# Spreading weight sums over chunks and moving the second transpose or hash behind the third pair of scores, in a hash-attention and feed-forward kernel

## The chip, the cores and the metric

One core of a Trainium2 chip. The metric is the device time of one execution in microseconds; medians of several runs are quoted.

PE is the matmul engine, PEld its weight load, DVE the vector engine, ACT the scalar engine, POOL GpSimd, SP the engine that issues most DMAs. In the views, `sc` are the scores, `tp_q` and `tp_k` the transposes of q and k, `hs` the hashes, `sm` the totals, `st` the transpose of the totals (L708), `accd` and `accp` the sums of probabilities on VectorE and on GpSimd, `pt` the exps.

## The reference, cut to what matters

```python
# q, k, v: (4, 8, 768, 64); proj: (64, 6); w_in (512, 2048), w_out (2048, 512)
mask   = q_bucket[:, :, :, None] == k_bucket[:, :, None, :]   # 6-bit hashes by proj
scores = where(mask, q @ k.T / sqrt(64), -1e9)
attn   = exp(scores - max);  attn /= sum(attn) + 1e-9
x      = (attn @ v) as (3072, 512)
h      = x @ w_in
out    = (max(h, 0) + alpha * min(h, 0)) @ w_out
```

## The kernel before: the parts that matter

Attention runs in 32 chunks `u` of 384 queries for a pair of heads. Beside its own work each chunk prepares one piece of the weights (`weight_*`, on DVE) and, for the next pair of heads, transposes (`turn`, even chunks) or hashes (`hash_bits`, odd chunks).

```python
    def weight_group(i):                     # every 4th piece of w_in, every 2nd of w_out
        ...
        for to, a, c in sums4:               # four sums in one block
            do(DVE.tensor_tensor(w[:, to], w[:, a], w[:, c], op=ALU.subtract))
        ... dma_start(w_in_s or w_out_s, w)

    def add_first(u):  do(POOL.tensor_tensor(accp[u], p(u, 0), p(u, 1), op=ALU.add))
    def add_third(u):  do(POOL.tensor_tensor(accp[u], accp[u], p(u, 2), op=ALU.add))
    def add_last(u):
        do(DVE.tensor_tensor(accd[u], p(u, 3), p(u, 4), op=ALU.add))        # L674
        do(DVE.tensor_tensor(accd[u], accd[u], p(u, 5), op=ALU.add))        # L675
        do(DVE.tensor_tensor(accd[u], accd[u], accp[u], op=ALU.add))        # L676

    for u in range(UNITS):
        scores(u, 0); add_first(u)
        if u > 0: add_last(u - 1)
        turn(pi+1,"q",0), turn(pi+1,"q",1)   or  hash_bits(pi+1, 0)
        if u > 0: attend(u - 1, 0)
        weight_parts(u)                      # L552 L553 L556 L557 on DVE
        scores(u, 1); add_third(u)
        weight_sum(u); weight_group(u)       # L577 L582, then the block L599
        turn(pi+1,"k",0), turn(pi+1,"k",1)   or  hash_bits(pi+1, 1)
        if u > 0: attend(u - 1, 1); totals(u - 1)
        scores(u, 2)
        if u > 0: divide(u - 1)              # begins with L708, the transpose of the totals
        load_weight(u + 3)
        if u == HW: load_w(0); load_w(1); load_x(0); sums_x(0)    # HW = 16; four sums on POOL
        ...
```

`turn`, `hash_bits` and `totals` take turns in two PSUM buffers named "mi"; one allocated to totals is free again when L708 has read it. The rest of the kernel (products with the feed-forward weights, after about 410 us) is not touched.

## Time and profile before

| | before |
|---|---|
| median | 997.81 us (997.47 to 998.15, 4 runs) |
| attention stage | about 20 to 410 us |
| DVE busy in chunks 1 to 15 | 170.37 of 178.83 us |
| PE busy in the same | 174.57 us |
| a chunk | 11.8 us, or 12.6 where a block of sums holds PE up |

What PE waits for, in the stage from 20 to 412 us (columns: total us, times, longest):

```profile
PE sm L698 <- DVE accd L676: 7.7, 6, 3.0
PE sc L653 <- ACT pt L658: 5.5, 30, 0.4
PE tp_q L614 <- DVE st L708: 2.7, 6, 0.6
```

Some 16 us in 390: PE's waits are small because PE is nearly full. And here are seven VectorE groups in that stage (busy us, mean ns; last the idle time before):

```profile
L676 DVE TENSOR_TENSOR accd<-accd,accp 128x768 f32<-128x768 f32 x32 | 53.4, 1667 | 3.3
L675 DVE TENSOR_TENSOR accd<-accd,pt 128x768 f32<-128x768 f32 x32 | 43.7, 1364 | 3.3
L674 DVE TENSOR_TENSOR accd<-pt,pt 128x768 f32<-128x768 f32 x32 | 40.3, 1260 | 0.0
L553 DVE TENSOR_SCALAR wx<-wx 128x512 uint32<-128x512 uint32 x31 | 35.9, 1158 | 1.1
L577 DVE SCALAR_TENSOR_TENSOR wr<-wx,wr 128x512 f32<-128x512 f32 x31 | 27.0, 872 | 1.1
L557 DVE SCALAR_TENSOR_TENSOR wr<-raw,wr 128x512 f32<-128x512 uint32 x31 | 23.0, 741 | 1.1
L556 DVE TENSOR_SCALAR wr<-wx 128x512 uint32<-128x512 uint32 x31 | 14.7, 475 | 1.1
```

These seven rows take 238.0 us, and the mean of the first four is far above the shortest of their kind. What is above it is time in which the engine counts as busy and stands still.

### The profile page before, as it was taken

Reading aid. Unit: us, or ns where it says so; the run is one execution under the profiler, and the core shown is the slowest. Engines: PE = TensorE matmul, PEld = TensorE weight load, DVE = VectorE, ACT = ScalarE, POOL = GpSimd, SP = SyncE. Lnnn points to the kernel's source line nnn. Section 1 sums busy time; section 2 is a strip of 40 time slices with the busy share of each in tenths; the row PEclk is TensorE's granted clock in tenths of the full one; section 3 lists DMA queues with packets and bytes.
Section 4 is the critical chain, followed back from the end, with each engine's and each line's share of the span. In section 5 each row is a group of like instructions: output and inputs, shape, how many; then the busy total and the mean of one; then the engine's idle time right before and its main releaser. Section 6 shows DMA issues by size and latency. Waiting matters only on the chain.

```text
span 998.3 us, 12489 instructions
## 1 busy us (share of the span) xinstructions
PE 963.2 (96%) x4741; PEld 594.0 (60%) x4741; DVE 605.8 (61%) x959; ACT 371.0 (37%) x669; POOL 158.5 (16%) x98
## 2 busy tenths in 40 slices
PE   6999999989999998999999999999999999999997
PEld 3444444434444443455788655888656888556886
DVE  3999999999999999766600366500467300665100
ACT  6777676665777664222100122100222000222000
POOL 2333333262333333000300000300000300000000
PEclk9999999998999999999999999999999999999999
DMA  7465756355444431463400133300224200231000
GB/s 199 126 182 143 237 154 179 107 164 157 143 143 143 127 111 53 200 259 110 137 22 22 58 111 99 123 22 21 71 88 155 68 22 22 84 111 37 22 22 24
DMA packets 93316, 106.81 MB, mean 107 GB/s; under 512 B 53296, under 2 KB 79936, under 8 KB 93248
## 3 DMA queue, kind: packets, MB, share of 16 engines
q1 hardware_dynamic: 91680, 105.54, 33.1%
q8 instruction: 39, 0.64, 0.3%
q10 hardware_dynamic: 1568, 0.39, 0.2%
q14 instruction: 29, 0.24, 0.1%
HBM read 78.65 MB, written 27.26 MB: 106 GB/s over the span
## 4 chain that ended last, share of the span: by engine, by line
PE 61%; DVE 35%; ACT 1%; issue 1%; DMA 1%; DVEq 0%; SPq 0%; ACTq 0%
PE z_2a L756 6%; PE z_1a L756 6%; PE z_0a L756 6%; DVE accd L676 5%; DVE accd L675 4%; DVE accd L674 4%; DVE wx L553 3%; PE z_1c L756 3%; PE z_0c L756 3%; PE z_2c L756 3%; DVE wr L577 2%; DVE wr L557 2%; PE f_2a L756 2%; PE f_3a L756 2%; PE f_7a L756 2%; PE f_6a L756 2%
## 5 line engine op out<-in xcount | busy, mean ns | idle before, releaser
L658 ACT ACTIVATE pt<-sc 128x768 f32<-128x768 f32 x192 | 149.9, 813 | 119.8 <-PE sc L653 119.8
L653 PE MATMUL sc<-qT,kT 64*128 64x384 f32 x768 | 157.5, 487 | 0.0
L686 PE MATMUL av<-pt,vn 128*64 128x385 f32 (+1 forms) x768 | 138.1, 495 | 0.0
L667 POOL TENSOR_TENSOR accp<-pt,pt 128x768 f32<-128x768 f32 x32 | 62.0, 1939 | 222.5 <-ACT pt L658 185.2
L686 PEld LDWEIGHTS av<-pt,vn 128*64 128x64 f32 x768 | 49.4, 136 | 72.6 <-issue 72.6
L732 POOL TENSOR_TENSOR x<-x,x 128x768 f32<-128x768 f32 x16 | 31.9, 2005 | 364.0 <-DMA x<-x_s 363.4
L810 DVE TENSOR_TENSOR g<-g,g 128x384 f32<-128x384 f32 x128 | 82.5, 665 | 2.2
L653 PEld LDWEIGHTS sc<-qT,kT 64*128 64x128 f32 x768 | 69.8, 190 | 15.3 <-issue 15.2
L653 PEld LDWEIGHTS <-kb 64*128 64x128 bf16 x384 | 24.4, 94 | 79.3 <-issue 62.7
L653 PE MATMUL sc<-qb,kb 64*128 64x384 bf16 x384 | 64.6, 329 | 5.6 <-ACT pt L658 5.6
L670 POOL TENSOR_TENSOR accp<-accp,pt 128x768 f32<-128x768 f32 x32 | 62.3, 1946 | 39.0 <-ACT pt L658 38.9
L756 PE MATMUL z_2a<-wo,g 128*128 128x256 f32 x256 | 58.0, 379 | 0.5 <-ACT z_2u L763 0.5
L756 PE MATMUL z_1a<-wo,g 128*128 128x256 f32 x256 | 57.9, 379 | 0.0
L756 PE MATMUL z_0a<-wo,g 128*128 128x256 f32 x256 | 57.9, 379 | 0.0
L676 DVE TENSOR_TENSOR accd<-accd,accp 128x768 f32<-128x768 f32 x32 | 53.4, 1667 | 3.3
L803 DVE SCALAR_TENSOR_TENSOR g<-h,alpha 128x384 f32<-128x384 f32 x32 | 22.1, 692 | 54.4 <-ACT h L795 54.4
L756 PEld LDWEIGHTS z_2a<-wo,g 128*128 128x128 f32 x256 | 48.6, 190 | 8.1 <-ACT z_2u L763 0.9
L756 PEld LDWEIGHTS z_0a<-wo,g 128*128 128x128 f32 x256 | 48.6, 190 | 7.5
L756 PEld LDWEIGHTS z_1a<-wo,g 128*128 128x128 f32 x256 | 48.6, 190 | 6.6
L675 DVE TENSOR_TENSOR accd<-accd,pt 128x768 f32<-128x768 f32 x32 | 43.7, 1364 | 3.3
L674 DVE TENSOR_TENSOR accd<-pt,pt 128x768 f32<-128x768 f32 x32 | 40.3, 1260 | 0.0
L639 ACT ACTIVATE qb<-hs,hb 32x384 bf16<-32x384 f32 x64 | 36.7, 574 | 2.2 <-PE hs L636 1.0
(217 smaller groups left out, 1477.1 us busy)
## 6 DMA issues: line engine op xcount, KB each, us to landing
wi<-w_in_s SPq DMA_DIRECT2D x32, 896.0 KB, 4.6
raw<-in_moe_w_in_dram SPq DMA_DIRECT2D x16, 512.0 KB, 4.1
raw<-in_moe_w_out_dram SPq DMA_DIRECT2D x16, 512.0 KB, 3.6
w_in_s<-wsi SPq DMA_DIRECT2D x16, 448.0 KB, 5.4
w_out_s<-wso SPq DMA_DIRECT2D x8, 896.0 KB, 4.4
wo<-w_out_s SPq DMA_DIRECT2D x8, 896.0 KB, 7.4
qn<-in_q_dram SPq DMA_DIRECT2D x32, 192.0 KB, 3.7
vn<-in_v_dram SPq DMA_DIRECT2D x16, 384.0 KB, 4.4
```

Of the source, the lines that this page charges most:

```text
L639: do(ACT.activation(bits["q", pi][D * s : D * s + 32, cols], ps[r], AF.Sign, bias=hb[r]))
L653: do(PE.matmul(sc[:, s, :CW], what["k", pi][r, ks], what["q", pi][r, qs], start=first, stop=not first,))
L658: do(ACT.activation(pt[:, :, :CW], sc[:, :, :CW], AF.Exp, scale=SCALE / DOWN))
L667: do(POOL.tensor_tensor(accp[u], p(u, 0), p(u, 1), op=ALU.add))
L670: do(POOL.tensor_tensor(accp[u], accp[u], p(u, 2), op=ALU.add))
L674: do(DVE.tensor_tensor(accd[u], p(u, 3), p(u, 4), op=ALU.add))
L675: do(DVE.tensor_tensor(accd[u], accd[u], p(u, 5), op=ALU.add))
L676: do(DVE.tensor_tensor(accd[u], accd[u], accp[u], op=ALU.add))
L686: do(PE.matmul(av[u][D * s : D * s + D, :w], nat["v", pi][:, s, kc * D : (kc + 1) * D], prob[u, kc][:, s, :w], start=(kc == 0), stop=(kc = ...
L732: do(POOL.tensor_tensor(x_m[b, to], x_m[b, a], x_m[b, c], op=ALU.subtract))
L756: do(PE.matmul(self.ps[bank], self.left(left, k), self.right(right, k), start=start and k == 0, stop=k == self.nk - 1, skip_group_check=no ...
L810: do(DVE.tensor_tensor(g_m[to, i], g_m[x, i], g_m[y, i], op=op))
```

## The change

The intent: no block of four sums that holds VectorE, and so L708 and PE, for 2.7 us at a time; and work for PE between the third pair of scores and the next chunk's first, where it waits for the exps.

```diff
+    sums_due = []
     def weight_group(i):
         ...
-        for to, a, c in sums4:
-            do(DVE.tensor_tensor(...))
-        ... dma_start(...)
+        for x in sums4:
+            sums_due.append((one, x))        # one(): the same tensor_tensor
+        sums_due.append((store, ()))         # store(): the same dma_start
+    def weight_sums(count):
+        while sums_due and (count or sums_due[0][0].__name__ == "store"):
+            fn, x = sums_due.pop(0)
+            count -= fn.__name__ == "one"
+            fn(*x)
@@ in the loop over chunks
         weight_sum(u)
+        weight_sums(1 if u < HW else 2)
         weight_group(u)
-        if more:
-            turn(pi + 1, "k", 0), turn(pi + 1, "k", 1)  or  hash_bits(pi + 1, 1)
         ... attend, totals, scores(u, 2), divide(u - 1)
+        if more:
+            turn(pi + 1, "k", 0), turn(pi + 1, "k", 1)  or  hash_bits(pi + 1, 1)
         load_weight(u + 3)
-        if u == HW:
+        if u == HW + 2:
             load_w(0); load_w(1); load_x(0); sums_x(0)
@@ after the loop
     divide(last)
+    weight_sums(4)
```

More of the change, by code (lines that the diff above doesn't have):

```diff
@@ L597, in weight_group, with one, store @@
             return
-        for to, a, c in sums4:
+        def one(to, a, c):
             do(DVE.tensor_tensor(w[:, to], w[:, a], w[:, c], op=ALU.subtract))
-        if i < HW:
-            c, kk = divmod(n, 2)
-            for ii in range(4):
-                nc.sync.dma_start(w_in_s[4 * c + ii][:, :, kk], w[:, :, ii])
-        else:
-            nc.sync.dma_start(w_out_s[n], w)
+        def store():
+            if i < HW:
+                c, kk = divmod(n, 2)
+                for ii in range(4):
+                    nc.sync.dma_start(w_in_s[4 * c + ii][:, :, kk], w[:, :, ii])
+            else:
+                nc.sync.dma_start(w_out_s[n], w)
+        for x in sums4:
[6 more added lines that the diff above has]
+            fn(*x)
     def turn(pi, name, half):
@@ L893, in fast_path @@
         weight_sum(u)
+        weight_sums(1 if u < HW else 2)
         weight_group(u)
-        if more:
-            if g == 0:
-                turn(pi + 1, "k", 0)
-                turn(pi + 1, "k", 1)
-            else:
-                hash_bits(pi + 1, 1)
         if u > 0:
@@ L908, in fast_path @@
             divide(u - 1)
+        if more:
+            if g == 0:
+                turn(pi + 1, "k", 0)
+                turn(pi + 1, "k", 1)
+            else:
+                hash_bits(pi + 1, 1)
         load_weight(u + 3)
-        if u == HW:
+        if u == HW + 2:
             load_w(0)
```

## The prediction

> **What bounds the kernel now.** I read the page's chain first, then busy time by stage, then the groups of VectorE (DVE), and last the timeline of a few chunks. A chunk (`u`, 32 of them) is half the queries of one pair of heads; even chunks transpose the next pair's q and k ("turn"), odd ones hash them.
>
> The chain that ended last, by engine:
>
> ```profile
> PE 61%; DVE 35%; ACT 1%; issue 1%; DMA 1%; DVEq 0%; SPq 0%; ACTq 0%
> ```
>
> 35% of 998 us is about 350 us, as long as the attention stage (from 20 to 410 us). Past 410 us the chain is matmuls back to back, and the change does nothing there. Busy time in four stretches of attention (columns: PE, PEld, DVE, ACT, POOL busy, granted clock, DMA share, GB/s); the second is the one where x is first loaded and summed:
>
> ```profile
> 25.27:204.10 178.83, 174.57 (x1168) 77.39 (x1166) 170.37 (x245) 127.94 (x212) 57.33 (x30) 1.00 0.56 160
> 204.10:246.66 42.56, 38.82 (x242) 17.17 (x240) 40.73 (x54) 24.37 (x42) 20.07 (x11) 0.92 0.55 163
> 246.66:391.85 145.19, 139.49 (x920) 60.37 (x918) 138.25 (x209) 99.00 (x162) 47.43 (x24) 1.00 0.40 126
> 391.85:412.00 20.15, 17.85 (x92) 7.43 (x89) 18.18 (x30) 4.14 (x6) 4.00 (x2) 1.00 0.17 66
> ```
>
> The first row is 15 chunks of 11.92 us, the third 12 chunks of 12.10. DVE and PE are both at 95% or more, so both are near the bound. DVE's busy time is not all work, though:
>
> ```profile
> L676 DVE TENSOR_TENSOR accd<-accd,accp 128x768 f32<-128x768 f32 x31 | 52.4, 1690 | 3.2
> L553 DVE TENSOR_SCALAR wx<-wx 128x512 uint32<-128x512 uint32 x31 | 35.9, 1158 | 1.1
> L599 DVE TENSOR_TENSOR wso<-wso 128x256 f32<-128x256 f32 x28 | 11.9, 425 | 1.0
> L599 DVE TENSOR_TENSOR wsi<-wsi 128x512 f32<-128x512 f32 x16 | 10.7, 691 | 0.4
> ```
>
> L676 has a mean of 1690 ns and L553 of 1158 ns, although single ones take 957 and 430. The timeline shows what stretches them, and where PE waits:
>
> ```profile
> 96.22 1.81 POOL L667 TENSOR_TENSOR accp<-pt,pt 128x768 f32<-128x768 f32 x1 [7.10 <-ACT pt L658]
> 96.30 2.54 DVE L676 TENSOR_TENSOR accd<-accd,accp 128x768 f32<-128x768 f32 x1
> ...
> 99.24 1.69 POOL L670 TENSOR_TENSOR accp<-accp,pt 128x768 f32<-128x768 f32 x1 [1.21 <-ACT pt L658]
> ...
> 99.48 1.73 DVE L553 TENSOR_SCALAR wx<-wx 128x512 uint32<-128x512 uint32 x1
> ...
> 103.88 2.75 DVE L599 TENSOR_TENSOR wsi<-wsi 128x512 f32<-128x512 f32 x4
> ...
> 104.39 0.34 PE L653 MATMUL sc<-qb,kb 64*128 64x384 bf16 x2 [0.17 <-ACT pt L658]
> ...
> 106.61 0.57 DVE L708 STREAM_TRANSPOSE st<-sm 128x384 f32<-128x384 f32 x1
> ...
> 107.24 0.55 PE L614 MATMUL tp_q<-ident,qn 128*128 128x128 f32 x3 [0.58 <-DVE st L708]
> ...
> 111.82 0.96 DVE L676 TENSOR_TENSOR accd<-accd,accp 128x768 f32<-128x768 f32 x1
> 111.85 2.47 POOL L670 TENSOR_TENSOR accp<-accp,pt 128x768 f32<-128x768 f32 x1 [2.02 <-ACT pt L658]
> ```
>
> L676, begun 0.08 us after a POOL sum, ends 0.81 us after that sum does: it stood still meanwhile. At 111.85 it is POOL that waits. At 103.88 the four sums of a weight group come as one block; the transpose L708, which frees a PSUM buffer, is late behind it, and PE stands 0.58 us. POOL's starts are 11.8 us apart in a chunk without sums and 12.6 us where a block of four delays PE. So the blocks cost 0.8 us per four chunks in the first half, and about that per two in the second.
>
> **What the Trainium skill says.** "SBUF — State Buffer", section "Who interferes with whom": VectorE and GpSimd share a port pair as an exclusive lock; a VectorE instruction with two SBUF inputs, or in a two-port mode, and a GpSimd instruction that reads SBUF block each other for the whole instruction, whichever came first. The trace agrees: L676 at 2.54 instead of 0.96 us, POOL's L670 at 2.47 instead of 1.69. "VectorE: DVE Perf Modes", section "Mode 2×_2P — use both read ports for one tensor": a tensor_scalar can use both ports; the trace agrees in that L553 stretches from 0.43 to 1.73. The weight sums have two SBUF inputs, so they belong to what can block; transposes and the division from PSUM do not. "TensorE: Matmul & The Clock Gate", section "What's actually happening": an idle window of about 3.4 us lowers the clock. In the second stretch, after PE idled 3.04 us, the granted clock averages 0.92.
>
> **The change part by part.** No matmul, no activation and no sum is removed or added (the order on the engines confirms it); three things move.
>
> (1) Sums one per chunk up to chunk 15, two afterwards. DVE keeps all 48 sums: four 512-wide ones in a block take 2.66 us plus 0.12 to enter, so 0.67 each; singly each pays the 0.12, 0.79 a chunk. In the second half two 256-wide cost 0.86 + 0.11 = 0.97 a chunk. That adds about 0.1 us a chunk on DVE and takes the block away.
>
> (2) The second turn or hash goes from between the second and third scores to behind the third. It gives ScalarE time between the third pair of scores and the next chunk's first, where PE now waits (0.17 shown, about 0.3 with the refilling). PE's pure time in a turn chunk, from distances between starts: scores 1.72, transposes 0.80, attend 2.09, scores 1.71, attend 1.99, totals 0.74, scores 1.72, transposes 0.88: 11.65 us. That is only 0.15 below the 11.8 of a chunk without sums.
>
> But the two rotating "mi" buffers now come in another order: q0, q1, totals, k0, k1 in a turn chunk, where it was q0, q1, k0, k1, totals. The built program shows that k1 now waits for this chunk's L708. PE comes to k1 0.74 + 1.72 + 0.40 = 2.9 us after it starts the totals, while before, in the chunk that starts at 104.39, L708 ended 3.4 us after that start (114.32 to 117.73); it stands behind the weight work, and now behind a sum too. Before, the transpose of q had the whole third pair and the next first pair as slack.
>
> (3) The first two loads of transformed w_in and of x are placed two chunks later, since the last w_in sums end in chunk 17. POOL's four sums of x (8.39 us) lock DVE as before, and I give this nothing. The last group's four sums come after the last division: 1.7 us less on DVE ahead of the first feed-forward products.
>
> Now DVE's own account. From one L708 to the next without stalls or sums is 8.97 us (128.36 to 140.00 is 11.64, of which L676 and L553 lost 2.71; plus half a 0.07). Before: four chunks take 48.04 (L676 at 96.30 and 144.34) = 4 × 8.97 + 2.78 + stalls, so 9.38 of stalls, 2.35 a chunk. After, I place the events by hand from L708 at 0, its next L676 at 4.35 and L553 at 5.94. In a hash chunk PE's k1 follows at 0.63, ScalarE's copy, abs, square and two exps end at 4.6, and POOL starts behind L676 at 5.15 and holds until 6.97: L553 loses 0.9. POOL's second sum falls into the L557 group and costs 1.5. In a turn chunk the same reckoning gives 1.25 and 1.5. The mean is 2.58 a chunk, as stalls do not vanish when sums are spread. So DVE needs 8.97 + 0.79 + 2.58 = 12.34 in the first half against 12.01, and 8.97 + 0.97 + 2.58 = 12.52 in the second against 12.2; PE would have only 11.65 and waits about 1.3 us at k1 of each turn chunk.
>
> Sum: 12 chunks × 0.33 = 4.0; 10 × 0.32 = 3.2; the w_in sums that slip into chunks 16 and 17, 1.5; the end, -1.7. That is +7, near 1004.6.
>
> **The rivals.** (A) PE becomes the only bound: DVE gets into a phase with fewer stalls and each chunk takes 11.65. Gain: 15 × 0.27 + 12 × 0.45 + 1.7 = 11 us, 986.5. For it: a block chunk of before lost only 1.6 us to POOL; the blocks visibly delay PE; the change is tuned like one that had been measured. Against: it needs stalls of 1.9 a chunk or less, and three of four chunks lose 2.2 to 2.8. (B) My main line, a new wait at k1 in place of the one at tp_q: 1004. (C) Stalls grow further, since POOL's two sums now come almost back to back and could catch L676 and L553 and L556 in turn: 3.1 a chunk, another 0.5 × 25 = 13 us, 1017. (D) The waits go below the clock gate's window somewhere else, or the lowered clock of about 7 us in the second stretch is avoided: plus or minus 3 us.
>
> **Range and chances.** The main line gets 0.55, A 0.33, C 0.1. My placement by hand has margins of 0.3 us against instructions of 1 to 2 us, so I shade the 1004.6 towards A: 1002. Range 987 to 1013. 2% is 20 us: faster would need 977.6, below PE's own floor, 0.02; slower needs 1017.5, C and something more, 0.05; within, 0.93.
>
> **What would show it.** Right: k1 (tp_k) waits for L708 by about a microsecond in every second chunk; the wait of scores on exps is gone; DVE stays at 95% with L676 shorter but L553, L556 and L557 longer; chunks of about 11.6 and 13.0 in turn; the sums single. Wrong: chunks evenly at 11.65 with DVE idle in places and fewer stalls (A), stalls over 3 us (C), or a gain in the stretch where x is summed, which I have at nothing.

## More of the kernel before

In the changed kernel the lines of interest have other numbers: L674 to L676 are L689 to L691, L708 is L723, the weight sums L599 are L602, POOL's L667 and L670 are L682 and L685. L552 to L582 keep theirs.

## The result, and the profile after

999.44 us median (999.23 to 1001.61, 4 runs) against 997.81 before. The ratio is 1.0021, interval 1.0004 to 1.0039. (Ratios are the mean time of one kernel's runs over that of the other's of the same rounds, so not quite the ratio of the medians.) Executions over 1.5% slower than the fastest of the same kernel are left out of the means. So the change is the same within 2%, if anything 2 us slower.

The chain by engine shows the same two engines as before, with VectorE's weight lines where the `accd` lines had been:

```profile
PE 59%; DVE 36%; DMA 1%; issue 1%; ACT 1%; DVEq 0%; SPq 0%; ACTq 0%
PE z_2a L771 6%; PE z_1a L771 6%; PE z_0a L771 6%; DVE wx L553 4%; DVE wr L557 4%; DVE wr L577 3%; DVE accd L691 3%; DVE wr L556 3%; DVE accd L690 3%; DVE accd L689 3%; PE z_1c L771 3%; PE z_0c L771 3%; PE z_2c L771 3%; PE f_3a L771 2%; PE f_2a L771 2%; PE f_7a L771 2%
```

The same seven groups after:

```profile
L553 DVE TENSOR_SCALAR wx<-wx 128x512 uint32<-128x512 uint32 x31 | 39.4, 1270 | 1.1
L557 DVE SCALAR_TENSOR_TENSOR wr<-raw,wr 128x512 f32<-128x512 uint32 x31 | 38.3, 1236 | 1.1
L577 DVE SCALAR_TENSOR_TENSOR wr<-wx,wr 128x512 f32<-128x512 f32 x32 | 36.2, 1130 | 1.1
L691 DVE TENSOR_TENSOR accd<-accd,accp 128x768 f32<-128x768 f32 x32 | 32.0, 999 | 3.3
L689 DVE TENSOR_TENSOR accd<-pt,pt 128x768 f32<-128x768 f32 x32 | 31.5, 983 | 0.0
L556 DVE TENSOR_SCALAR wr<-wx 128x512 uint32<-128x512 uint32 x31 | 31.1, 1003 | 1.1
L690 DVE TENSOR_TENSOR accd<-accd,pt 128x768 f32<-128x768 f32 x32 | 30.7, 958 | 3.4 <-ACT pt L673 0.2
```

The three `accd` sums went from 137.4 us to 94.2, almost their bare time (3 x 32 x 0.957 = 91.9). The four weight rows went from 100.6 to 145.0. The total is 239.2 against 238.0 (one L577 more lies in the window). The stalls did not shrink. They moved from one group of instructions to another, because POOL's two sums now start at another point of VectorE's round.

The timeline of two chunks shows how (start, length, engine, line, what, idle time before it):

```profile
93.18 0.58 DVE L723 STREAM_TRANSPOSE st<-sm 128x384 f32<-128x384 f32 x1
...
93.81 0.55 PE L629 MATMUL tp_k<-ident,kn 128*128 128x128 f32 x3 [0.79 <-DVE st L723]
...
97.52 0.96 DVE L691 TENSOR_TENSOR accd<-accd,accp 128x768 f32<-128x768 f32 x1
97.74 2.41 POOL L682 TENSOR_TENSOR accp<-pt,pt 128x768 f32<-128x768 f32 x1 [7.55 <-ACT pt L673]
...
99.12 1.32 DVE L553 TENSOR_SCALAR wx<-wx 128x512 uint32<-128x512 uint32 x1
...
100.94 2.22 DVE L557 SCALAR_TENSOR_TENSOR wr<-raw,wr 128x512 f32<-128x512 uint32 x1
...
105.20 0.57 DVE L723 STREAM_TRANSPOSE st<-sm 128x384 f32<-128x384 f32 x1
...
111.14 1.67 DVE L553 TENSOR_SCALAR wx<-wx 128x512 uint32<-128x512 uint32 x1
...
112.84 1.79 DVE L556 TENSOR_SCALAR wr<-wx 128x512 uint32<-128x512 uint32 x1
...
117.33 0.58 DVE L723 STREAM_TRANSPOSE st<-sm 128x384 f32<-128x384 f32 x1
```

In the hash chunk (93 to 105) POOL's first sum comes just after L691 has begun and waits for it, so L691 escapes. L553 then loses 1.32 - 0.43 = 0.89 us and L557 2.22 - 0.69 = 1.53. In the turn chunk (105 to 117) L553 loses 1.24 and L556 1.36. That is 2.5 us a chunk. The two chunks take 24.15 us from L723 to L723. Before, four took 48.04.

What PE waits for, from 20 to 412 us:

```profile
PE tp_k L629 <- DVE st L723: 16.8, 11, 7.4
PE sm L713 <- DVE accd L691: 1.2, 1, 1.2
PE sc L668 <- ACT pt L673: 0.4, 2, 0.3
```

The wait of the scores on the exps is gone (5.5 to 0.4) and that on `accd` nearly so, but the transposes of k now wait for L723, for 16.8 us, and 7.4 of it once, in chunk 18 with the four POOL sums of x. The total is 18 us where it was 16. VectorE itself waits for 1.5 us in these 392 before the change and for 3.6 after it: it has less slack than PE in both.

Where the time came from, by POOL's first sum of a chunk, which both traces have:

| stretch | before | after | difference |
|---|---|---|---|
| start to chunk 4 | 60.77 | 63.32 | +2.55 |
| chunks 4 to 15 | 143.33 | 144.00 | +0.67 |
| chunks 16 to 18, with the sums of x | 42.56 | 43.41 | +0.85 |
| chunks 19 to 28 | 121.72 | 121.58 | -0.14 |
| chunks 29 and 30 | 23.47 | 21.44 | -2.03 |
| chunk 31 and the rest | 606.45 | 605.95 | -0.50 |
| sum | 998.3 | 999.7 | +1.4 |

The cuts need care. Chunk 19 still bears the sums of x (13.68 us, against 11.81 before): with it, chunks 16 to 19 cost +2.7, and chunks 20 to 27 gain 0.8. And POOL's mark stands at another place of a chunk after the change. By PE's start of the totals, the stretch from chunk 29's to the end takes 611.45 us against 612.00, so most of the -2.5 in the rows of chunks 29 to 31 is a shift of the mark.

The first row is a surprise. In chunk 0 ScalarE, not PE, is late, and the turn of k used to fill PE's wait there. With it moved, PE stands idle, and in this trace the clock falls. Busy time and granted clock (the last but two column) from 16 to 20 and from 20 to 24 us, after:

```profile
16.00:20.00 4.00, 1.64 (x14) 0.89 (x12) 3.34 (x6) 4.00 (x9) 2.07 (x2) 1.00 0.28 64
20.00:24.00 4.00, 4.00 (x20) 2.34 (x19) 3.79 (x4) 2.62 (x5) 1.57 (x1) 0.57 0.55 120
```

and before:

```profile
16.00:20.00 4.00, 2.56 (x20) 1.45 (x18) 3.38 (x7) 4.00 (x9) 2.09 (x2) 1.00 0.31 71
20.00:24.00 4.00, 3.63 (x30) 1.72 (x26) 3.87 (x3) 4.00 (x9) 1.50 (x1) 1.00 0.51 116
```

4 us at 0.57 of the clock is 1.7 us lost to the clock: part of the pause was filled before, and is not after. But the pause does not always lower the clock. x_at_hw, an experiment below that does the same in chunk 0, has the same wait and keeps the full clock:

```profile
19.63 0.34 PE L668 MATMUL sc<-qb,kb 64*128 64x384 bf16 x2 [2.37 <-ACT pt L673]
20.00:24.00 4.00, 4.00 (x32) 2.14 (x32) 3.86 (x4) 3.63 (x7) 1.55 (x1) 1.00 0.55 113
```

Its chunk 4 begins at 61.73 us, where the changed kernel has 63.32. So 1.6 of the +2.55 us belong to this one execution. Of the eight traces with this turn moved in whole or in half, three show the fall (0.57 here, 0.59 in half_turn, 0.61 in dve_place_only); of the six without, none.

### The profile page after: what moved, and what is told of

Its sections match the earlier page's. It is cut to its first block, busy times and chain, and to the rows that moved or that the text cites. A ratio compares the mean times of both kernels' runs of the same rounds, so it can differ in the third digit from the quotient of the medians.

```text
span 999.7 us, 12487 instructions
## 1 busy us (share of the span) xinstructions
PE 960.9 (96%) x4741; PEld 591.6 (59%) x4741; DVE 606.5 (61%) x959; ACT 373.1 (37%) x669; POOL 158.9 (16%) x98
## 4 chain that ended last, share of the span: by engine, by line
PE 59%; DVE 36%; DMA 1%; issue 1%; ACT 1%; DVEq 0%; SPq 0%; ACTq 0%
PE z_2a L771 6%; PE z_1a L771 6%; PE z_0a L771 6%; DVE wx L553 4%; DVE wr L557 4%; DVE wr L577 3%; DVE accd L691 3%; DVE wr L556 3%; DVE accd L690 3%; DVE accd L689 3%; PE z_1c L771 3%; PE z_0c L771 3%; PE z_2c L771 3%; PE f_3a L771 2%; PE f_2a L771 2%; PE f_7a L771 2%
## 5 line engine op out<-in xcount | busy, mean ns | idle before, releaser
L682 POOL TENSOR_TENSOR accp<-pt,pt 128x768 f32<-128x768 f32 x32 | 65.9, 2058 | 245.4 <-ACT pt L673 245.4
L685 POOL TENSOR_TENSOR accp<-accp,pt 128x768 f32<-128x768 f32 x32 | 58.6, 1830 | 17.7 <-DVE wr L556 9.2
L668 PEld LDWEIGHTS <-kb 64*128 64x128 bf16 x384 | 19.1, 94 | 66.7 <-issue 53.6
L553 DVE TENSOR_SCALAR wx<-wx 128x512 uint32<-128x512 uint32 x32 | 40.2, 1257 | 1.1
L557 DVE SCALAR_TENSOR_TENSOR wr<-raw,wr 128x512 f32<-128x512 uint32 x32 | 39.0, 1219 | 1.1
L577 DVE SCALAR_TENSOR_TENSOR wr<-wx,wr 128x512 f32<-128x512 f32 x32 | 36.2, 1130 | 1.1
```

What stands on the lines that cost most here:

```text
L553: do(DVE.tensor_scalar(x.bitcast(U32), x.bitcast(U32), 3, 0xC0000000, op0=ALU.logical_shift_left, op1=ALU.bitwise_xor,))
L557: do(DVE.scalar_tensor_tensor(r, lo, 2.0 ** -52, r, op0=ALU.mult, op1=ALU.mult))
L577: do(DVE.scalar_tensor_tensor(r, x, -1.0 if turned else 1.0, r, op0=ALU.mult, op1=ALU.subtract if turned else ALU.add,))
L668: do(PE.matmul(sc[:, s, :CW], what["k", pi][r, ks], what["q", pi][r, qs], start=first, stop=not first,))
```

## The experiments

Theory 1, the one of the prediction: in attention VectorE's own work plus its stalls on the lock with GpSimd set each chunk, and PE's waits follow from it. Theory 2: PE's waits (for L708 or L723, for the exps, behind blocks of sums) set the time, and VectorE's stalls only fill slack. Twelve kernels ran in three sets, each set against the kernel before on the same chip (medians of before: 999.35, 999.12, 998.89).

| run | median us | ratio to before | interval |
|---|---|---|---|
| the change itself (its own set) | 999.44 | 1.0021 | 1.0004 to 1.0039 |
| sums_only | 999.58 | 1.0003 | 0.9989 to 1.0017 |
| place_only | 1001.77 | 1.0025 | 1.0011 to 1.0038 |
| half_turn | 999.34 | 0.9999 | 0.9986 to 1.0013 |
| start_old | 999.07 | 1.0000 | 0.9987 to 1.0014 |
| one_pool_after (wrong result) | 984.0 | 0.9848 | 0.9833 to 0.9863 |
| one_pool_before (wrong result) | 984.5 | 0.9859 | 0.9844 to 0.9875 |
| dve_adds_after | 983.34 | 0.9854 | 0.9836 to 0.9872 |
| dve_adds_before | 990.33 | 0.9911 | 0.9895 to 0.9927 |
| dve_sums_only | 984.79 | 0.9858 | 0.9843 to 0.9873 |
| dve_place_only | 989.14 | 0.9902 | 0.9886 to 0.9917 |
| third_on_dve | 994.28 | 0.9957 | 0.9942 to 0.9972 |
| x_at_hw | 999.71 | 1.0009 | 0.9996 to 1.0023 |

### Each part alone: sums_only and place_only

```diff
# sums_only: the changed kernel, but
         weight_group(u)
+        turn k / second hash              # back in its old place
...
         divide(u - 1)
-        turn k / second hash
# place_only: the kernel before with only that block moved the other way
```

> The changed kernel's sums, taken one or two per chunk, with the turn and hash in their old place. Theory 1 (VectorE's own work plus its stalls on the lock with GpSimd set each chunk; PE's waits only follow): spreading removes little, for the stalls stay at 2.3 to 2.8 us a chunk: 998 to 1008 us, chunks about 12.0 to 12.4 us, VectorE still 95% busy. Theory 2 (the blocks of four sums delay PE, and PE sets the time otherwise): every chunk falls to 11.8 us, 988 to 992 us.

> The sums in blocks as in the kernel before, the second turn or hash behind the third scores. Theory 1: four chunks need 4 x 8.97 + 2.78 of work plus four times about 2.5 us of stalls, 48.7 us against 48.0 before: 999 to 1005 us, with the wait of tp_k for the transpose L708 of about 1 us in each turn chunk. Theory 2: the wait of the scores on the exps goes (0.3 us a chunk), the blocks keep costing: 985 to 992 us.

sums_only came out at 1.0003. Its halves differ. POOL's first sums in an early and a late stretch:

```profile
84.34 1.89 POOL L682 TENSOR_TENSOR accp<-pt,pt 128x768 f32<-128x768 f32 x1 [6.95 <-ACT pt L673]
...
96.16 1.85 POOL L682 TENSOR_TENSOR accp<-pt,pt 128x768 f32<-128x768 f32 x1 [6.92 <-ACT pt L673]
```

```profile
268.50 1.82 POOL L682 TENSOR_TENSOR accp<-pt,pt 128x768 f32<-128x768 f32 x1 [7.34 <-ACT pt L673]
...
281.09 1.82 POOL L682 TENSOR_TENSOR accp<-pt,pt 128x768 f32<-128x768 f32 x1 [7.34 <-ACT pt L673]
...
293.69 1.81 POOL L682 TENSOR_TENSOR accp<-pt,pt 128x768 f32<-128x768 f32 x1 [7.36 <-ACT pt L673]
```

With one sum a chunk every chunk takes 11.8 us, as Theory 2 had it, and the blocks' delay is gone. With two a chunk every one takes 12.6, where before one in two did. Two sums are only 0.19 us more work than one, but the stalls are larger too: 12.6 - 8.97 - 0.79 = 2.8 us a chunk against 11.8 - 8.97 - 0.60 = 2.2 (VectorE's bare time is the 8.97 of the prediction). The phase between POOL and VectorE is another one. place_only at 1.0025 is what Theory 1 expected, and the opposite of Theory 2: its tp_k wait for L708 is 16.9 us, its median 2.4 above that of before. Neither part alone gives anything.

### The new wait itself: half_turn

```diff
# the changed kernel, but
         weight_group(u)
+        if more and g == 0: turn(pi + 1, "k", 1)     # ahead of the totals
...
-            turn(pi + 1, "k", 0), turn(pi + 1, "k", 1)
+            turn(pi + 1, "k", 0)                     # alone behind the third scores
```

> The changed kernel, but of the turn of k the second half stays ahead of the totals and only the first goes behind the third scores, so that the PSUM buffer which waits for L708 is wanted 2 us later. Theory 1: the tp_k wait (16.8 us in all) vanishes or reappears elsewhere and the time stays within 3 us of the changed kernel, 997 to 1002 us, as VectorE has as much to do. Theory 2 (the tp_k wait costs what it shows): 10 of its 11 waits of 0.8 to 1.5 us come off, 985 to 990 us.

(The edit also lets `turn` make its tile at its first call, whichever half that is.)

The wait of tp_k for the transpose is gone from the trace, and 15 us of others stand in its place:

```profile
PE hs L651 <- DVE st L723: 7.5, 3, 7.1
PE sm L713 <- DVE accd L691: 6.9, 7, 2.8
```

The time is 0.9999 of before: at most 2 us better than the changed kernel, where the intervals overlap, and not the 10 or more that the wait showed. PE waits for VectorE in whatever place the buffers put it. The wait is a symptom.

### The first chunk: start_old

```diff
# the changed kernel, but
         weight_group(u)
+        if u == 0: turn(pi + 1, "k", 0), turn(pi + 1, "k", 1)
...
-        if more:
+        if more and u > 0:
```

> The changed kernel, but in chunk 0 alone the turn of k stays between the second and third scores. In the trace the changed kernel has lost 1.9 us by the second chunk's first GpSimd sum and 2.6 us by the fifth's, while it gains 2 us after chunk 19. If the first chunk's placement is what lost it: 1.5 to 2.5 us faster than the changed kernel, about 997 us. If the loss comes from the later chunks: no difference, 999 to 1000 us.

In its trace the second chunk's POOL sum starts at 25.60 us, where the changed kernel has 27.17, and the fifth's at 61.65 against 63.32. The granted clock from 20 to 24 us is 1.00. But x_at_hw, with the moved turn, reaches the fifth chunk at 61.73 with the clock at 1.00 too, so these 1.6 us are the clock of the one execution that was profiled, and the placement itself costs nothing there that shows. The median, 999.07, is no faster than 999 to 1000 us, the second of the two expectations; the ratio (1.0000 against 1.0021, of different sets) is within the intervals. Whether the moved turn makes the fall of the clock more likely stays open.

### Less lock: one_pool_after and one_pool_before

```diff
 def add_third(u):
-    do(POOL.tensor_tensor(accp[u], accp[u], p(u, 2), op=ALU.add))
+    pass                     # wrong on purpose: a third block of keys missing
```

> The changed kernel without GpSimd's second sum of each chunk (wrong result on purpose: the third block of keys is missing from the totals). VectorE's own work is unchanged, one lock of GpSimd per chunk is gone. Theory 1: about 1.3 us of stalls a chunk go, and chunks fall until PE's own 11.65 us holds them: 0.4 us x 31, 985 to 989 us. Theory 2 (the lock only fills VectorE's slack): within 3 us of the changed kernel.

> The kernel before without GpSimd's second sum of each chunk (wrong result on purpose). Theory 1: the chunks delayed by blocks of four sums recover, all go to about 11.8 us (PE with its 0.3 us wait on the exps): 988 to 992 us, so 2 to 5 us slower than the changed kernel with the same cut, which shows what the new placement would give PE if VectorE let it. Theory 2: within 3 us of the kernel before.

VectorE's program is the same to the instruction, it waited for no POOL result before, and both kernels are 1.4 to 1.5% faster than the kernel before. VectorE now waits for PE's totals, 13.6 us in one_pool_after and 19.0 in one_pool_before, from 20 to 400 us. So POOL's sums hold VectorE up, and that is on the path; Theory 2's "slack" is out. The chunks of one_pool_after take half of 108.32 - 85.17, or 11.58 us, PE's own time (the prediction had 11.65):

```profile
85.17 2.00 POOL L682 TENSOR_TENSOR accp<-pt,pt 128x768 f32<-128x768 f32 x1 [10.79 <-ACT pt L673]
95.72 1.82 POOL L682 TENSOR_TENSOR accp<-pt,pt 128x768 f32<-128x768 f32 x1 [8.55 <-ACT pt L673]
108.32 1.98 POOL L682 TENSOR_TENSOR accp<-pt,pt 128x768 f32<-128x768 f32 x1 [10.78 <-ACT pt L673]
```

Those of one_pool_before take 11.80 (84.47 to 96.28, and 108.06 to 119.91), with its wait on the exps. That is the 0.2 us a chunk that the new placement gives PE. My expectation of 2 to 5 us between the two failed all the same: they are 0.5 us apart, and both below their ranges. By PE's start of the totals, the chunks with the x sums (15 to 20: 65.02 us against 61.33 in one_pool_before, with a wait of 4.8 us at tp_k) and the stretch from chunk 29 to the end (609.74 against 608.24) take it back.

### No lock: dve_adds_after and dve_adds_before

```diff
-def add_first(u): POOL sum;  def add_third(u): POOL sum
 def add_last(u):
     do(DVE.tensor_tensor(accd[u], p(u, 3), p(u, 4), op=ALU.add))
     do(DVE.tensor_tensor(accd[u], accd[u], p(u, 5), op=ALU.add))
-    do(DVE.tensor_tensor(accd[u], accd[u], accp[u], op=ALU.add))
+    for kc in (0, 1, 2):
+        do(DVE.tensor_tensor(accd[u], accd[u], p(u, kc), op=ALU.add))
```

> The changed kernel with all sums of probabilities on VectorE, none on GpSimd in this stage but for x: two more sums of 1.05 us a chunk for VectorE, in place of 2.5 us of stalls. Correct result. Theory 1: VectorE needs 8.97 + 0.6 + 2.1 = 11.7 us a chunk against 12.1 now, about PE's own 11.65: 985 to 991 us. Theory 2 (VectorE's work is what counts, stalls are slack): 2.1 us more work a chunk, slower, 1010 us or more.

> The kernel before with all sums of probabilities on VectorE. Correct result. Theory 1: 8.97 + 0.7 + 2.1 = 11.8 us a chunk on the mean, but blocks of four sums still delay PE in some chunks: 988 to 996 us, slower than the changed kernel with the same edit by 1 to 6 us. Theory 2: slower than before, 1010 us or more.

Giving the fuller engine two more instructions a chunk brings the changed kernel 1.5% and the unchanged one 0.9% below the kernel before: 983.34 and 990.33 us, both correct. The first is below its range of 985 to 991 us, and the two are 7.0 us apart, where I expected 1 to 6. In dve_adds_after the same lines of VectorE are (20 to 412 us):

```profile
L691 DVE TENSOR_TENSOR accd<-accd,pt 128x768 f32<-128x768 f32 x96 | 92.0, 958 | 3.3
...
L557 DVE SCALAR_TENSOR_TENSOR wr<-raw,wr 128x512 f32<-128x512 uint32 x31 | 21.5, 693 | 1.1
L577 DVE SCALAR_TENSOR_TENSOR wr<-wx,wr 128x512 f32<-128x512 f32 x31 | 21.4, 692 | 1.1
...
L556 DVE TENSOR_SCALAR wr<-wx 128x512 uint32<-128x512 uint32 x31 | 14.7, 476 | 1.1
L553 DVE TENSOR_SCALAR wx<-wx 128x512 uint32<-128x512 uint32 x31 | 13.2, 427 | 1.1
```

The four weight rows fall from 145.0 us to 70.8. This is what the stalls were: the seven rows of the changed kernel at these bare times would be 91.9 + 70.8 = 162.7, so 239.2 - 162.7 = 76.5 us of them were stalls, and 75.3 before (3 to 5 of both are due to the sums of x, which hold an instruction of VectorE for about 1.5 us each). POOL's 64 sums, done by VectorE, cost it 64 x 0.958 = 61.3. Handing them to POOL cost the fuller engine more than keeping them.

Not all of the gain comes from this. Without sums of its own in the chunks, POOL also does the four sums of x earlier, at 74 and 125 us, where the changed kernel has them at 236:

```profile
74.39 1.93 POOL L747 TENSOR_TENSOR x<-x,x 128x768 f32<-128x768 f32 x1 [71.42 <-DMA x<-x_s]
124.94 6.29 POOL L747 TENSOR_TENSOR x<-x,x 128x768 f32<-128x768 f32 x3 [48.63 <-DMA x<-x_s]
```

This holds for all four runs without the lock. Stretches from PE's start of one chunk's totals to that of another's, in us:

| stretch | before | after | dve_adds_before | dve_adds_after | dve_sums_only | dve_place_only |
|---|---|---|---|---|---|---|
| start to 3 | 66.27 | 66.78 | 66.70 | 65.48 | 66.92 | 67.09 |
| 3 to 15 | 144.14 | 144.00 | 143.77 | 141.04 | 141.86 | 143.62 |
| 15 to 20 | 65.72 | 68.94 | 58.97 | 58.94 | 58.98 | 58.82 |
| 20 to 29 | 110.17 | 108.53 | 104.76 | 104.43 | 104.60 | 105.40 |
| 29 to the end | 612.00 | 611.45 | 614.20 | 611.61 | 610.84 | 612.37 |

From 20 to 29 no sum of x falls in any of them: there 108.53 becomes 104.43, or 12.06 us a chunk 11.60, and 110.17 becomes 104.76. That part is the 64 sums. But 10.0 of the 18.2 us between the traces of dve_adds_after and the changed kernel lie from 15 to 20, where the sums of x were; they cost less in their new place, and no run separates the two.

### Which part is worth what without the lock: dve_sums_only and dve_place_only

The edit is that of the last section, on sums_only and on place_only.

> All sums of probabilities on VectorE, weight sums from the queue, turn and hash in their old place. With the lock gone VectorE needs about 11.5 to 11.7 us a chunk, so PE's order should decide: with its wait of 0.3 us on the exps a chunk takes 11.8, 986 to 991 us, nearer to the kernel before with this edit (990.3) than to the changed one (983.3). If the spreading of the sums is what the 7 us between those two come from: 982 to 985 us.

> All sums of probabilities on VectorE, weight sums in blocks, the second turn or hash behind the third scores. If the placement is what the 7 us come from: 983 to 986 us; if the spreading is: 988 to 991 us. A block falls in odd chunks, whose transpose L708 is wanted late, so I expect the first.

I expected the placement to be what the 7 us between 983.3 and 990.3 come from. It was the queue of sums: dve_sums_only 0.9858, next to both parts' 0.9854, and dve_place_only 0.9902, next to neither's 0.9911. Without the lock, the queue is worth about 0.5% and the placement less than the intervals tell. With the lock, the queue's gain does not appear. The table shows where it lies: of the 5.2 us between the traces of dve_adds_before and dve_sums_only, 3.4 come after chunk 29's totals, where the last sums are late, and 1.9 from 3 to 15, where the sums of x now fall; from 20 to 29 the two differ by 0.2. So the chunks in between gain nothing from spreading.

### One of two sums: third_on_dve

```diff
 def add_third(u): pass
 def add_last(u):
     ... accd += accp
+    do(DVE.tensor_tensor(accd[u], accd[u], p(u, 2), op=ALU.add))
```

> The changed kernel with only GpSimd's second sum of each chunk moved to VectorE, the first left. Correct result. If each GpSimd sum costs VectorE about 1.25 us of stalls and doing it itself costs 1.05: 8.97 + 0.6 + 1.05 + 1.25 = 11.9 us a chunk, between the changed kernel (12.1) and all on VectorE (11.5): 989 to 995 us. If stalls are slack: 1005 us or more.

994.28 us, within the range: between none and both, as a cost per POOL sum has it.

### The sums of x: x_at_hw

```diff
+        if u == HW:
+            load_x(0); sums_x(0)
         if u == HW + 2:
-            load_w(0); load_w(1); load_x(0); sums_x(0)
+            load_w(0); load_w(1)
```

> The changed kernel with the load of x and its four GpSimd sums back at chunk 16, the loads of w_in at 18. In the trace the wait of tp_k for L708 is 7.4 us once, in the chunk of these sums. If those sums cost the same wherever they stand, as predicted: within 1.5 us of the changed kernel, 998 to 1001 us, and the 7.4 us wait moves to chunk 16. If their new place costs: 2 to 4 us faster.

1.0009 against the change's 1.0021, with overlapping intervals; its tp_k wait is 17.0 us in all with the longest at 7.6, now at 220 us, in chunk 16. So the place of these sums makes no difference that can be told.

## Why the prediction was right or wrong, point by point

- **The bound** was right. VectorE stays at 95% in attention (136.62 of 143.02 us after chunk 19); with fewer stalls the time falls, and with the PE wait moved it does not.
- **The new wait at k1** was right: tp_k waits for L723 by 0.8 to 1.0 us, in most of the turn chunks. The wait on the exps vanished as said.
- **Where the lock would bite** was right almost to the instruction: 0.9 at L553 and 1.5 at L557 in a hash chunk were measured as 0.89 and 1.53, 1.25 and 1.5 in a turn chunk as 1.24 and 1.36, the second at L556.
- **The size of a single sum** was wrong, and it is the largest term that made +7 out of +1.6. I took 0.79 us for a single 512-wide sum and 0.97 for two 256-wide ones. They take 0.60 (92.58 to 93.18) and 0.79 (305.82 to 306.61). A block of four took 2.78, so four single ones save 0.4 us instead of losing. The kernel's text gives a likely reason, which no run tested: in the block three of the four read what one of the two instructions ahead of them wrote, while a sum from the queue reads tiles that were complete earlier. 0.19 less in 12 chunks and 0.18 in 10 is 4.1 us of the overshoot; the stalls, 2.51 instead of 2.58, are another 1.5. Chunks 4 to 15 and 19 to 28 were to cost +7.2 and cost +0.5; the later ones, once free of the sums of x (20 to 27), even gained 0.8.
- **The start** was not in the sum. The moved turn of chunk 0 opens a pause of PE. In the profiled execution the clock then fell, which is 1.6 of the +2.55 us by chunk 4; in x_at_hw it did not.
- **The end** was put at -1.7, for the four late sums, and came to -2.5 by POOL's mark (chunks 29 and 30, then the rest). The late sums are not the reason: place_only, which has none, shows -2.3 by the same mark, and sums_only, which has them, +0.1. By PE's totals the changed kernel gains 0.55 there, so the number came near by luck.
- **Chunks 16 to 18** were put at +1.5, for the w_in sums that slip, and cost +0.85, or +2.7 with chunk 19. The slip is not the reason: from chunk 16 to 20 sums_only, which has it, takes 53.49 us and place_only, which has not, 57.11, against 54.37 before. So it is the placement that makes the sums of x dearer, which the prediction gave nothing; that they cost the same in chunk 16 as in 18 held (x_at_hw, 56.45 against 57.09).
- **Rival A**, a phase with fewer stalls at PE's own pace, did occur for one half in one experiment (sums_only, 11.8 us a chunk), not in the changed kernel. Shading 1004.6 towards it brought the 1002 nearer to the 999.44, so part of the closeness is luck.

Of the Trainium skill, what "SBUF — State Buffer" says in "Who interferes with whom", that the second to issue fully blocks, is what the traces here show: POOL's sum at 97.74, begun 0.22 us after L691, ends 1.67 us after L691 does. "Perfetto Trace Analysis", in "Optimizing Scalar/DVE Operations", says that offloading between GpSimd and VectorE "might not help"; here it cost 0.9% in the kernel before (990.33 against 999.12) and 1.6% in the changed one (983.34 against 999.44, of another set), the moved sums of x included. "TensorE: Matmul & The Clock Gate", section "What's actually happening", says that the window in which PE's activity is watched runs freely, whatever the kernel does. That the same pause of 2.37 us in chunk 0 was followed by 0.57 in one trace and by 1.00 in another agrees with it; no run here shows the window itself.

## What to carry to other kernels

Where GpSimd and VectorE both read SBUF, count a GpSimd sum against VectorE as stall time before calling it offloaded: here 64 of them cost some 70 us of stalls and 61 us when VectorE did them itself. Rearranging the order on an engine that stalls on a lock can move the stalls to other instructions and leave their sum as it was (75 us before, 76 after). When an experiment takes an engine's work away, look at what else that engine then does at another time (here the sums of x), and read the gain in a stretch that is free of it. A difference at one place of one trace needs a second trace of the same program before it has a cause. A wait that appears in a trace is worth its length only if removing it leaves nothing else to wait for.

The version that beats both kernels is the changed one with all sums of probabilities on VectorE, 983.34 us.

## What the Trainium skill lacked or had wrong

- "SBUF — State Buffer", section "Who interferes with whom", gives the rule of the lock but no reckoning of what an offloaded instruction then costs. Here a GpSimd sum of 128x768 fp32 cost VectorE about 1.1 to 1.2 us of stalls (70 to 75 us by 64), and VectorE does it in 0.96.
- "VectorE: DVE Perf Modes", section "The DRAIN you can't avoid", reports a chain of copies that takes as long with a semaphore after each as without, though it adds that an instruction that is not held starts earlier. Here a sum that reads what the instruction ahead of it wrote starts 0.73 us after that one's start (103.15 to 103.88), and one that reads nothing just written 0.61 (91.97 to 92.58), behind the same instruction of the same length, 0.69.
- "TensorE: Matmul & The Clock Gate" speaks of idle windows of about 3.4 us, and not of shorter pauses. Here one recorded wait of PE of 2.37 us (idle from 17.3 to 19.7 us) was followed by 4 us at 0.57 of the clock in one trace, and at 1.00 in x_at_hw, place_only and three more with the same wait; in half_turn, whose longest wait there is 1.28 us, 0.59 followed.
